# Batches in every eighth row: a decode block with x and biases in one transfer, merged VectorE copies and two weight pieces over eight DMA engines

## The chip, the cores and the metric

The kernel runs on one core of a Trainium2 chip. The metric is the time of one execution on the device in microseconds (us), lower is better. Before the change it is 214.59 us, the median of three runs (214.52 to 214.60).

## What is computed

One decode step of a transformer block, all in float32: attention over the last 1024 positions of a cache, with grouped query heads, and then an MLP, each behind a layer norm. The batch is B = 4, the model width D = 448, with 16 query heads on 8 key/value heads of 256, and F = 1792.

```python
def _A_ref(x, k_cache, v_cache, wq, wo):      # x: (4, 1, 448)
    W = min(4096, max(256, Sk // 4))          # 1024
    rep = Hq // Hkv                           # 2
    q = ((x @ wq).reshape(B, Sq, Hq, Dh)).transpose(0, 2, 1, 3)
    k = jnp.repeat(k_cache[:, :, Sk - W:, :], rep, axis=1)
    v = jnp.repeat(v_cache[:, :, Sk - W:, :], rep, axis=1)
    p = _softmax(jnp.einsum("bhqd,bhkd->bhqk", q, k) * (Dh ** -0.5), axis=-1)
    o = jnp.einsum("bhqk,bhkd->bhqd", p, v)
    return o.transpose(0, 2, 1, 3).reshape(B, Sq, Hq * Dh) @ wo

def _B_ref(x, w1, b1, w2, b2):
    y = _layernorm(x, axis=-1)
    h = _gelu(jnp.einsum("bsd,df->bsf", y, w1) + b1)
    return jnp.einsum("bsf,fd->bsd", h, w2) + b2

h = x + _A_ref(_layernorm(x, axis=-1), A_k_cache, A_v_cache, A_wq, A_wo)
h2 = h + _B_ref(_layernorm(h, axis=-1), B_w1, B_b1, B_w2, B_b2)
```

Some 88 MB are read for it: the windows of the two caches (67 MB) and the weights.

## The kernel before

**Tiles and stages.** The work goes by the eight key/value heads, called groups g0 to g7. For a group there is one k tile and one v tile of 128 partitions by 9984 floats: 8192 columns of cache, and behind them 1792 columns of weights, so that cache and weights come in one transfer. The k tile of group g carries the query weights of group g+1, the v tile the output weights of group g. Both kinds have two buffers (`ring`, line 37), so a load waits until the tile two before it is done with. The first v buffer takes `wq0` (the query weights of group 0, with x); the last k buffers take w1 and w2.

**A group's path.** `project_q` (L156) multiplies the normed x by the query weights and transposes the result (L165); VectorE reduces it and copies it to `qT` (L167, L173). `scores` (L175) multiplies `qT` with k into two halves of PSUM, VectorE takes the maxima (L186) and makes `nm`, the negative scaled maximum (L189, L190); ScalarE does the exponentials (L194). `transpose_p` (L203) turns them and VectorE copies them to `pT` (L211). `values` (L216) multiplies by v, `transposed_output` (L234) scales, transposes and folds the result into `oT` (L243, L244), and `add_output` (L246) adds the group's share of the output projection into `acc`. The main loop (L280 to L290) runs one group ahead with the scores.

**The tail.** From L293 on come the last group's value product in pieces, the residual and the two norms, the first MLP matmuls `pu` (L388), the gelu, and the second MLP: `pa` (L421) and `py` (L431). w2 comes in three pieces of 8, 4 and 2 row blocks; `py` starts with the second piece and ends with the third. `res` (L437) adds the residual, and one store writes the output. Matmuls on a zero tile (`keep_warm`) stand between them.

**Where batches lie.** PSUM results have four quadrants of 32 rows (Q = 32) for four concurrent matmuls. Of each quadrant only the first B = 4 rows hold a batch. The x rows and biases (`rs`, L129 to L133) are loaded into these rows by four transfers of 4 rows each, issued by ScalarE.

**The last 64 query rows.** The weights have 448 rows: three blocks of 128 and one of 64. In a packed weight tile the block of 64 rows by 512 columns stands as 128 rows by 256 columns. For group 1 alone it doesn't: k0 carries 1536 columns of weights, and the block comes in two transfers of 32 rows by 512 floats (L73) into `wq1_last`. Its source has 8 outer elements of four rows each, followed by padding, so that the outermost dimension of the transfer is 8.

**What sets the order.** PE's order is that of the code (`manual_schedule`). All bulk loads are issued by SyncE (SP) on one queue, q1, in the order of the program; a load waits for its buffer and for the semaphore lane that it takes over from an earlier transfer (eight lanes in turn, over both queues). ScalarE issues the `rs` rows on queue q10. Queues q8 and q14 fetch instructions.

Of the kernel before, what the change touches and what calls it, by code (L numbers as in the profile page):

```python
# [8 lines left out]
F32 = mybir.dt.float32  # L9
BF16 = mybir.dt.bfloat16  # L10
AF = mybir.ActivationFunctionType
ALU = mybir.AluOpType
# [14 lines left out]
Q = 32  # L27
CACHE = NKC * B * DH
WEIGHTS = 4 * D
EPS = 1e-5  # L30
SCALE = DH ** -0.5

@with_exitstack
def block_kernel(ctx: ExitStack, tc, rows, wq0, k0, wq1, kq, vo, w1, w2, out):
# [13 lines left out]
    def load(kind, src, pieces, name):  # L48
        t = ring.tile([P, CACHE + WEIGHTS], F32, tag=kind, name=name)
        at = 0  # L50
        for n in pieces:
            nc.sync.dma_start(t[:, at : at + n], src[:, at : at + n])  # L52
            at += n
        return t
# [8 lines left out]
        return parts  # L63


    def load_k(g):
        half = CACHE // 2
        if g == 0:
            t = load("k", k0, (CACHE + 3 * 512,), "k0")


            for i in range(2):
                nc.sync.dma_start(  # L73
                    wq1_last[i * Q : (i + 1) * Q, :], wq1[i].rearrange("e (p c) -> e p c", c=512)[:, :4, :]
                )
# [18 lines left out]
    ident = const.tile([P, P], F32, name="ident")  # L94
# [11 lines left out]

    yT = const.tile([P, ND + 1, Q], F32, name="yT")
    nc.vector.memset(yT, 0.0)
    wq1_last = const.tile([H, 512], F32, name="wq1_last")
    zT = const.tile([P, ND, Q], F32, name="zT")  # L110
    nc.vector.memset(zT, 0.0)

# [6 lines left out]
    rows_of = ident.rearrange("p (j q) -> p j q", j=4)[:, :, :B]  # L119
# [8 lines left out]

    rs = const.tile([P, 2 * P + FQ], F32, name="rs")  # L129
    nc.gpsimd.memset(rs, 0.0)  # L130
    for j in range(4):
        nc.scalar.dma_start(rs[j * Q : j * Q + B, :], rows[j])
    xb, b2b, b1b = rs[:, :P], rs[:, P : 2 * P], rs[:, 2 * P :]  # L133


# [20 lines left out]
    def project_q(g, parts):  # L156
        pq = ps_m.tile([P, 512], F32, tag="m", name=f"pq{g}")
        for j, y, cols, w in parts:
            nc.tensor.matmul(pq[j * Q : (j + 1) * Q, cols], y, w, start=True, stop=True)  # L159
        qs = work.tile([P, 512], F32, tag="qs", name=f"qs{g}")  # L160
        nc.scalar.copy(qs, pq)  # L161

        pt = ps_m.tile([P, 2 * REP, P], F32, tag="m", name=f"pqt{g}")
        for i in range(2 * REP):
            nc.tensor.transpose(pt[:, i, :], qs[:, i * P : (i + 1) * P], ident)  # L165
        sm = work.tile([P, 2 * REP, B], F32, tag="sm", name=f"sm{g}")
        nc.vector.tensor_reduce(  # L167
            sm, pt.rearrange("p i (j q) -> p i q j", j=4)[:, :, :B, :], axis=AX.X, op=ALU.add
        )

        src = sm.rearrange("p (r c) b -> p c b r", r=REP)
        for i in range(2):
            nc.vector.tensor_copy(qT[g % 2][:, :, :, i * REP : (i + 1) * REP], src)  # L173

    def scores(g, kt):  # L175
        mx = work.tile([P, 2], F32, tag="mx", name=f"mx{g}")
        halves = []
        for h in range(2):
            s = ps_s.tile([P, 512], F32, tag="s", name=f"s{g}_{h}")
            for c in range(2):  # L180
                for b in range(B):
                    nc.tensor.matmul(  # L182
                        s[b * Q : (b + 1) * Q, :], qT[g % 2][:, c, b, :], kt[h][:, c, b, :],
                        start=(c == 0), stop=(c == 1),
                    )
# [4 lines left out]
        nc.vector.tensor_scalar_mul(nm, nm, -SCALE)  # L190
# [12 lines left out]
    def transpose_p(g, p):  # L203
        for h in range(2):
            pt = ps_t.tile([P, 4, P], F32, tag="t", name=f"ppt{g}_{h}")
            for c in range(4):
                nc.tensor.transpose(pt[:, c, :], p[:, (4 * h + c) * P : (4 * h + c + 1) * P], ident)  # L207

            src = pt.rearrange("p (c i) (b q) -> p c i b q", i=2, b=B)
            for i in range(2):  # L210
                nc.vector.tensor_copy(  # L211
                    pT[g % 2][:, 2 * h : 2 * h + 2, :, i * REP : (i + 1) * REP], src[:, :, i, :, :REP]
                )


    def values(g, vt, po, pairs=range(NKC // 2)):  # L216
# [17 lines left out]
    def transposed_output(g, po, rec):  # L234
        o = work.tile([P, 2, DH], F32, tag="o", name=f"o{g}")
        nc.vector.tensor_scalar_mul(o, po, rec)  # L236
        pt = ps_m.tile([P, 2, 2, P], F32, tag="m", name=f"pot{g}")
        for i in range(2):
            for c in range(2):
                nc.tensor.transpose(pt[:, i, c], o[:, i, c * P : (c + 1) * P], ident)  # L240
        dst = oT[g % 2].rearrange("p (r c) q -> p c r q", r=REP)[:, :, :, :B]
# [51 lines left out]
    g = HKV - 2  # L293
# [88 lines left out]
    pu = ps_s.tile([P, 512], F32, tag="s", name="pu")[:, :FQ]  # L382
    pv = ps_m.tile([P, 2], F32, tag="m", name="pv")
    for a in range(ND):
        m = Q if a == 0 else B
        for j in range(4):
            rows, w = w1_part(a, j)
            nc.tensor.matmul(  # L388
                pu[j * Q : j * Q + m, :], zT[rows, a, :m], w, start=(a == 0), stop=(a == ND - 1),
            )  # L390
        if a == 0:
            rsqrt(r1, row_mean(dv, pv[:, 0:1], "v1"), "r1")
        if a == 1:
            v2 = stat("v2")
            nc.vector.tensor_scalar(v2, row_mean(zv, pv[:, 1:2], "v2"), r1, r1, op0=ALU.mult, op1=ALU.mult)
            rsqrt(s, v2, "r2")
            nc.vector.tensor_mul(s, s, r1)
# [10 lines left out]
    for rows in (slice(0, H), slice(H, P)):  # L408
        nc.tensor.matmul(put[rows, 3], u[:, 3 * P :], rows_of, start=True, stop=True)
    dst = gT[:, :12, :].rearrange("p (c j) q -> p c j q", c=3)  # L410
    nc.vector.tensor_copy(dst[:, :, :, :B], put[:, :3])

    for i, rows in enumerate((slice(0, H), slice(H, P))):
        nc.scalar.copy(gT[rows, 12:, :B], put[rows, 3].rearrange("p (j i) q -> p j i q", i=2)[:, :, i, :])
    keep_warm(1, warm)

    first = 8
    pa = ps_w.tile([P, D], F32, tag="acc", name="pa")
    for c in range(first):
        j, m = c % 4, Q if c < 4 else B  # L420
        nc.tensor.matmul(  # L421
            pa[j * Q : j * Q + m, :], gT[:, c, :m], w2t[c], start=(c < 4), stop=(c >= first - 4),
        )
    pas = once.tile([P, D], F32, tag="u", name="pas")
    nc.scalar.copy(pas, pa)
    py = ps_o.tile([P, 2, H], F32, tag="o", name="py")
    for c in range(first, NFC):
        for j in range(4):
            m, n = (Q, 2) if c == first else (B, 2 if j < 3 else 1)
            w = columns(w2t[c], j) if n == 2 else w2t[c][:, None, 3 * P :]  # L430
            nc.tensor.matmul(  # L431
                py[j * Q : j * Q + m, :n, :], gT[:, c, :m], w, start=(c == first), stop=(c == NFC - 1),
            )
        if c == first + 1:
            add_quadrants(py, pas, False)
# [69 lines left out]
```

## Time and profile before

| what | value |
|---|---|
| median time of three runs | 214.59 us |
| span of the profiled execution (first to last instruction) | 212.9 us |
| time that lies around that span | 1.69 us |
| PE busy | 137.9 us (65%) |
| VectorE (DVE) busy | 39.2 us (18%), 167 instructions |
| ScalarE (ACT) busy | 21.0 us (10%) |
| moved by DMA | 88.46 MB, mean 415 GB/s |
| mean granted TensorE clock | 0.872 |

The slices of the page cut the span into 40 parts of 5.3 us. A line of a group reads: source line, engine, operation, output<-input, shapes, count, then busy us and mean ns of one, then the idle time before them and what ended it. In a chain, the entry "DMA w<-w" is the time from what preceded it to the landing of that transfer. For each execution there is one span and the times of all queues' packets; the sixteen DMA engines are not told apart in any view.

### The profile page before, as it was taken

The page shows a single profiled execution, that of the slowest core. Times are in us where ns is not written, and L with a number is a line of the kernel's source. Part 1 is how long each engine was busy: PE and PEld are TensorE (multiplying, and loading weights), DVE is VectorE, ACT ScalarE, POOL GpSimd, SP SyncE. Part 2 cuts the span into 40 slices and gives each one's busy share as a digit, 9 for nine tenths or more (in the row PEclk, how much of TensorE's full clock was granted, in tenths as well). Part 3 has the DMA queues.
Part 4 walks back from the last instruction along what each step waited for, and adds up shares of the span by engine and source line. Part 5 has one row for each costly group of instructions (what it writes and reads, how often), then busy time and mean ns, then how long its engine had stood idle before and what let it go on. Part 6 is the DMA issues. An engine that isn't in the chain of part 4 may idle for free.

```text
span 212.9 us, 2306 instructions
## 1 busy us (share of the span) xinstructions
PE 137.9 (65%) x971; PEld 49.1 (23%) x971; DVE 39.2 (18%) x167; ACT 21.0 (10%) x52; POOL 5.6 (3%) x17
## 2 busy tenths in 40 slices
PE   0456868093886739583986348382948476798994
PEld 0322233021231212211231113120222123234432
DVE  1420324001130202210130104110230231022320
ACT  0210213000030000300030003000030001000311
POOL 6100000000000000000000000000000000000110
PEclk9999999669597966969599859979797999699999
DMA  7999998999989999999999999999989999999991
GB/s 291 426 399 469 398 465 378 459 465 390 458 378 465 465 390 458 398 446 465 390 458 405 443 465 386 465 413 428 461 375 468 440 428 390 417 418 433 424 390 60
DMA packets 3865, 88.46 MB, mean 415 GB/s; under 512 B 448, under 2 KB 576, under 8 KB 1168
## 3 DMA queue, kind: packets, MB, share of 16 engines
q1 hardware_dynamic: 3824, 88.29, 96.9%
q8 instruction: 7, 0.11, 0.2%
q10 hardware_dynamic: 32, 0.05, 0.1%
q14 instruction: 2, 0.02, 0.0%
HBM read 88.26 MB, written 0.07 MB: 415 GB/s over the span
## 4 chain that ended last, share of the span: by engine, by line
DMA 85%; PE 11%; DVE 2%; issue 0%; SPq 0%
DMA v<-vo 65%; DMA w<-w 12%; DMA k<-k 8%; PE po L219 8%; PE acc L248 1%; DVE o L236 1%; PE pot L240 1%; PE py L431 1%; DVE oT L243 0%; DVE oT L244 0%; SPq L52 0%; DVE res L437 0%; PE py L256 0%
## 5 line engine op out<-in xcount | busy, mean ns | idle before, releaser
L182 PE MATMUL s<-k,qT 128*32 128x512 f32 x256 | 42.3, 822 | 24.7 <-DMA k<-kq 22.6
L219 PE MATMUL po<-v,pT 128*32 128x512 f32 x256 | 40.0, 772 | 19.6 <-DMA v<-vo 19.6
L186 DVE TENSOR_REDUCE mx<-s 128x1 f32<-128x512 f32 x16 | 11.1, 691 | 67.4 <-PE s L182 67.4
L182 PEld LDWEIGHTS s<-k,qT 128*32 128x32 f32 x256 | 10.0, 146 | 54.7 <-issue 29.4
L219 PEld LDWEIGHTS po<-v,pT 128*32 128x32 f32 x256 | 10.7, 135 | 42.3 <-issue 31.4
L161 ACT COPY qs<-pq 128x512 f32<-128x512 f32 x8 | 4.7, 586 | 135.8 <-PE pq L159 135.8
L236 DVE TENSOR_SCALAR o<-po,rec 128x512 f32<-128x512 f32 x8 | 6.0, 750 | 60.2 <-PE po L219 60.2
L194 ACT ACTIVATE p<-s,nm 128x512 f32<-128x512 f32 x16 | 10.9, 690 | 18.4 <-DVE nm L190 18.4
L207 PE MATMUL ppt<-ident,p 128*128 128x128 f32 x64 | 10.5, 286 | 2.0 <-ACT p L194 1.7
L165 PE MATMUL pqt<-ident,qs 128*128 128x128 f32 x32 | 5.7, 304 | 6.2 <-ACT qs L161 6.2
L240 PE MATMUL pot<-ident,o 128*128 128x128 f32 x32 | 5.2, 286 | 5.7 <-DVE o L236 5.7
L248 PE MATMUL acc<-v,oT 128*32 128x448 f32 x56 | 6.7, 551 | 3.3 <-DVE oT L244 3.3
L207 PEld LDWEIGHTS ppt<-ident,p 128*128 128x128 f32 x64 | 6.7, 140 | 6.0 <-ACT p L194 6.0
L159 PE MATMUL pq<-k,yT 128*32 128x512 f32 (+1 forms) x66 | 7.3, 515 | 0.0
L308 PE MATMUL warm<-idle 128*32 128x512 bf16 x25 | 7.3, 382 | 0.0
L240 PEld LDWEIGHTS pot<-ident,o 128*128 128x128 f32 x32 | 3.3, 140 | 13.0 <-DVE o L236 13.0
L165 PEld LDWEIGHTS pqt<-ident,qs 128*128 128x128 f32 x32 | 3.6, 150 | 10.9 <-ACT qs L161 9.1
L153 POOL TENSOR_TENSOR r<-ve_r,mhalf 128x1 f32<-128x1 f32 x2 | 1.1, 544 | 191.9 <-DVE ve_r L152 191.9
L211 DVE COPY pT<-ppt 128x16 f32<-128x16 f32 x32 | 4.7, 170 | 4.7 <-PE ppt L207 4.7
L159 PEld LDWEIGHTS pq<-k,yT 128*32 128x32 f32 x66 | 3.1, 110 | 6.1 <-issue 4.8
L138 PE MATMUL pm_x<-wq,mean 128*128 128x12 f32 x2 | 0.6, 363 | 5.8 <-DMA wq<-wq 5.8
L167 DVE TENSOR_REDUCE sm<-pqt 128x16 f32<-128x64 f32 x8 | 1.8, 225 | 13.0 <-PE pqt L165 13.0
(101 smaller groups left out, 60.9 us busy)
## 6 DMA issues: line engine op xcount, KB each, us to landing
v<-vo SPq DMA_DIRECT2D x7, 4992.0 KB, 31.8
k<-kq SPq DMA_DIRECT2D x6, 4992.0 KB, 32.0
k<-k SPq DMA_DIRECT2D x1, 4864.0 KB, 16.3
k<-kq SPq DMA_DIRECT2D x1, 4096.0 KB
w<-w SPq DMA_DIRECT2D x2, 1792.0 KB
v<-vo SPq DMA_DIRECT2D x2, 1024.0 KB, 22.2
v<-vo SPq DMA_DIRECT2D x1, 2048.0 KB
w<-w SPq DMA_DIRECT2D x1, 1344.0 KB
```

The lines of the kernel that those rows point to most:

```text
L159: nc.tensor.matmul(pq[j * Q : (j + 1) * Q, cols], y, w, start=True, stop=True)
L161: nc.scalar.copy(qs, pq)
L165: nc.tensor.transpose(pt[:, i, :], qs[:, i * P : (i + 1) * P], ident)
L182: nc.tensor.matmul(s[b * Q : (b + 1) * Q, :], qT[g % 2][:, c, b, :], kt[h][:, c, b, :], start=(c == 0), stop=(c == 1),)
L186: nc.vector.reduce_max(mx[:, h : h + 1], s, axis=AX.X)
L194: nc.scalar.activation(p[:, h * 512 : (h + 1) * 512], halves[h], AF.Exp, bias=nm, scale=SCALE, accum_out=sums[:, h : h + 1],)
L207: nc.tensor.transpose(pt[:, c, :], p[:, (4 * h + c) * P : (4 * h + c + 1) * P], ident)
L219: nc.tensor.matmul(po[b * Q : (b + 1) * Q], pT[g % 2][:, c, b, :], vt[c][:, :, b, :], start=(c == 0), stop=(c == NKC // 2 - 1),)
L236: nc.vector.tensor_scalar_mul(o, po, rec)
L240: nc.tensor.transpose(pt[:, i, c], o[:, i, c * P : (c + 1) * P], ident)
L248: nc.tensor.matmul(acc[i * Q : (i + 1) * Q, :], oT[g % 2][:, i, :], wt[:, i, :], start=(g == 0), stop=(g == HKV - 2),)
L308: nc.tensor.matmul(warm[:Q], idle[:, :Q], idle, start=True, stop=True)
```

## The change

Batch b now lies in row 8b of its quadrant instead of row b (STEP = 8), for `rs`, `oT`, `zT`, `gT`, and the selection from `ident`. With that, the sixteen rows of x and biases are one regular transfer. `qT`, `nm` and `pT` are made with one VectorE instruction where there were two. In the tail, matmuls that used 4 columns of weights use 32. And the last 64 query rows of group 2 leave k1 and come like those of group 1, through an outermost dimension of 8.

```diff
@@ load_k
+    def load_last(n):
+        t = wq_last[:, n, :]
+        for i in range(2):
+            nc.sync.dma_start(
+                t[i * Q : (i + 1) * Q, :], wql[n, i].rearrange("e (p c) -> e p c", c=512)[:, :4, :]
+            )
+        return t
...
-            last = wq1_last
+            last = load_last(0)
+        elif g == 1:
+            t = load("k", kq[0], (CACHE + 3 * 512,), "k1")
+            last = load_last(1)
...
-    for j in range(4):
-        nc.scalar.dma_start(rs[j * Q : j * Q + B, :], rows[j])
+    nc.scalar.dma_start(rs[::STEP, :], rows)
@@ project_q, scores, transpose_p
-        src = sm.rearrange("p (r c) b -> p c b r", r=REP)
-        for i in range(2):
-            nc.vector.tensor_copy(qT[g % 2][:, :, :, i * REP : (i + 1) * REP], src)
+        src = sm.rearrange("p (r c) b -> p c b r", r=REP)[:, :, :, None, :].to_broadcast([P, 2, B, 2, REP])
+        nc.vector.tensor_copy(qT[g % 2][:, :, :, : 2 * REP].rearrange("p c b (i r) -> p c b i r", i=2), src)
...
-        nc.vector.tensor_max(nm, mx[:, 0:1], mx[:, 1:2])
-        nc.vector.tensor_scalar_mul(nm, nm, -SCALE)
+        nc.vector.tensor_scalar(nm, mx[:, 0:1], mx[:, 1:2], -SCALE, op0=ALU.max, op1=ALU.mult)
...
-            src = pt.rearrange("p (c i) (b q) -> p c i b q", i=2, b=B)
-            for i in range(2):
-                nc.vector.tensor_copy(
-                    pT[g % 2][:, 2 * h : 2 * h + 2, :, i * REP : (i + 1) * REP], src[:, :, i, :, :REP]
-                )
+            src = pt.rearrange("p (c i) (b q) -> p c b i q", i=2, b=B)[:, :, :, :, :REP]
+            dst = pT[g % 2][:, 2 * h : 2 * h + 2, :, : 2 * REP]
+            nc.vector.tensor_copy(dst.rearrange("p c b (i r) -> p c b i r", i=2), src)
@@ the rows of a batch, here zT; oT, gT and rows_of likewise
-    nc.vector.tensor_copy(zT[:, :, :B], pz)
+    nc.vector.tensor_copy(zT[:, :, ::STEP], pz)
@@ the tail, here pu; pa and py likewise
-        m = Q if a == 0 else B
...
-                pu[j * Q : j * Q + m, :], zT[rows, a, :m], w, start=(a == 0), stop=(a == ND - 1),
+                pu[j * Q : (j + 1) * Q, :], zT[rows, a, :], w, start=(a == 0), stop=(a == ND - 1),
```

On SyncE, the first loads of the program before were these; `wq` is group 0's weights with x, a lane is named DMAHW with its number, and PE and DVE stand for a wait for a buffer's readers:

```order
L52 DMA wq_134<-wq 128x1808
L52 DMA k_174<-k 128x9728
L73 DMA wq_last<-wq 32x1x512 x2
L52 DMA k_239<-kq 128x9984 [waits DMAHW0_49]
L52 DMA v_241<-vo 128x9984 [waits DMAHW1_49]
L52 DMA k_335<-kq 128x9984 [waits DMAHW2_49,PE_49]
L52 DMA v_337<-vo 128x9984 [waits DMAHW3_49,DVE_49]
```

And now:

```order
L53 DMA wq_131<-wq 128x1808
L53 DMA k_170<-k 128x9728
L70 DMA wq_last<-wql 32x1x512 x2
L53 DMA k_231<-kq 128x9728
L70 DMA wq_last<-wql 32x1x512 x2
L53 DMA v_235<-vo 128x9984 [waits DMAHW0_49]
L53 DMA k_324<-kq 128x9984 [waits DMAHW1_49,PE_49]
L53 DMA v_326<-vo 128x9984 [waits DMAHW2_49,DVE_49]
```

Two transfers have moved in between k1 and v0, k1 has 256 columns less and waits for no lane, and v0 waits for the lane of `wq0` instead of that of k0.

On VectorE, the work between two groups' maxima, here of group 1, before:

```order
L189 TENSOR_TENSOR nm_264<-mx_243 128x1
L190 TENSOR_SCALAR nm_264<-nm_264 128x1
L167 TENSOR_REDUCE sm_287<-pqt_282 128x16
L173 COPY qT_111<-sm_287 128x8x2 x2
L211 COPY pT_114<-ppt_0_291 128x8x2
L199 TENSOR_TENSOR rec_271<-sums_268 128x1
L211 COPY pT_114<-ppt_0_291 128x8x2
L200 RECIPROCAL rec_271<-rec_271 128x1
L211 COPY pT_114<-ppt_1_298 128x8x2 x2
```

And now:

```order
L196 TENSOR_SCALAR nm_258<-mx_237 128x1
L175 TENSOR_REDUCE sm_279<-pqt_274 128x16
L180 COPY qT_111<-sm_279 128x8x4
L217 COPY pT_114<-ppt_0_282 128x8x4
L205 TENSOR_TENSOR rec_264<-sums_261 128x1
L206 RECIPROCAL rec_264<-rec_264 128x1
L217 COPY pT_114<-ppt_1_288 128x8x4
```

Eleven instructions (two rows stand for two each) have become seven, in the same order.

On PE, the last matmuls of the tail kept their number and order; the weights of `py` before and now, in the first rows:

```order
L431 MATMUL py<-w_827,gT 32x128 x4
L431 MATMUL py<-w_827,gT 4x128 x3
L431 MATMUL py<-w_827,gT 4x64
L256 MATMUL py<-pas,sel 32x128 x4
L431 MATMUL py<-w_827,gT 4x128 x3
L431 MATMUL py<-w_827,gT 4x64
```

```order
L434 MATMUL py<-w_796,gT 32x128 x7
L434 MATMUL py<-w_796,gT 32x64
L260 MATMUL py<-pas,sel 32x128 x4
L434 MATMUL py<-w_796,gT 32x128 x3
L434 MATMUL py<-w_796,gT 32x64
```

Only the width of a weight tile has changed, from 4 to 32 columns.

More of the change, by code (lines that the diff above doesn't have):

```diff
@@ L27 @@
 Q = 32
+STEP = Q // B
 CACHE = NKC * B * DH
@@ L33, in block_kernel @@
 @with_exitstack
-def block_kernel(ctx: ExitStack, tc, rows, wq0, k0, wq1, kq, vo, w1, w2, out):
+def block_kernel(ctx: ExitStack, tc, rows, wq0, k0, wql, kq, vo, w1, w2, out):
     nc = tc.nc
@@ L108, in block_kernel @@
     nc.vector.memset(yT, 0.0)
-    wq1_last = const.tile([H, 512], F32, name="wq1_last")
+    wq_last = const.tile([H, 2, 512], F32, name="wq_last")
     zT = const.tile([P, ND, Q], F32, name="zT")
@@ L118, in block_kernel @@
     fold = fold.rearrange("p j q -> p (j q)")
-    rows_of = ident.rearrange("p (j q) -> p j q", j=4)[:, :, :B]
+    rows_of = ident.rearrange("p (j q) -> p j q", j=4)[:, :, ::STEP]
     qT = [const.tile([P, 2, B, Q], F32, name=f"qT{i}") for i in range(2)]
@@ L410, in block_kernel @@
     dst = gT[:, :12, :].rearrange("p (c j) q -> p c j q", c=3)
-    nc.vector.tensor_copy(dst[:, :, :, :B], put[:, :3])
+    nc.vector.tensor_copy(dst[:, :, :, ::STEP], put[:, :3])
     for i, rows in enumerate((slice(0, H), slice(H, P))):
-        nc.scalar.copy(gT[rows, 12:, :B], put[rows, 3].rearrange("p (j i) q -> p j i q", i=2)[:, :, i, :])
+        nc.scalar.copy(gT[rows, 12:, ::STEP], put[rows, 3].rearrange("p (j i) q -> p j i q", i=2)[:, :, i, :])
     keep_warm(1, warm)
@@ L419, in block_kernel @@
     for c in range(first):
-        j, m = c % 4, Q if c < 4 else B
+        j = c % 4
         nc.tensor.matmul(
-            pa[j * Q : j * Q + m, :], gT[:, c, :m], w2t[c], start=(c < 4), stop=(c >= first - 4),
+            pa[j * Q : (j + 1) * Q, :], gT[:, c, :], w2t[c], start=(c < 4), stop=(c >= first - 4),
         )
@@ L428, in block_kernel @@
         for j in range(4):
-            m, n = (Q, 2) if c == first else (B, 2 if j < 3 else 1)
+            n = 2 if c == first or j < 3 else 1
             w = columns(w2t[c], j) if n == 2 else w2t[c][:, None, 3 * P :]
             nc.tensor.matmul(
-                py[j * Q : j * Q + m, :n, :], gT[:, c, :m], w, start=(c == first), stop=(c == NFC - 1),
+                py[j * Q : (j + 1) * Q, :n, :], gT[:, c, :], w, start=(c == first), stop=(c == NFC - 1),
             )
@@ L488 @@
     rows = np.concatenate([quadrants(xp), quadrants(b2), quadrants(np.asarray(B_b1).reshape(1, F))], axis=2)
+    rows = rows.reshape(4 * B, 2 * P + FQ)
     arrays = {
-        "rows": rows, "wq0": np.concatenate([wq[0], xT], axis=1), "k0": k0, "wq1": wq1, "kq": kq, "vo": vo, "w1": w1, "w2": w2,
+        "rows": rows, "wq0": np.concatenate([wq[0], xT], axis=1), "k0": k0, "wql": wql, "kq": kq, "vo": vo, "w1": w1, "w2": w2,
     }
@@ L502 @@
     r = run(nc, [arrays], core_ids=[0])
-    got = np.asarray(r.results[0]["out"]).reshape(4, Q, P)[:, :B, :]
+    got = np.asarray(r.results[0]["out"]).reshape(4, B, STEP, P)[:, :, 0]
     return np.ascontiguousarray(got.transpose(1, 0, 2).reshape(B, 1, 4 * P)[:, :, :D])
```

10 lines of the change are left out of this document (3 added, 7 removed).

## The prediction

> **What bounds the kernel now.** I read the page's busy shares and slices first, then the queues, then the chain.
>
> ```profile
> span 212.9 us, 2306 instructions
> DMA  7999998999989999999999999999989999999991
> q1 hardware_dynamic: 3824, 88.29, 96.9%
> q8 instruction: 7, 0.11, 0.2%
> q10 hardware_dynamic: 32, 0.05, 0.1%
> q14 instruction: 2, 0.02, 0.0%
> DMA 85%; PE 11%; DVE 2%; issue 0%; SPq 0%
> ```
>
> The sixteen DMA engines are busy in every slice from the second to the last but one, and 85% of the chain that ended last is DMA. SyncE's queue q1 alone fills 96.9% of the sixteen engines' span. One engine therefore moves 88.29 MB / (0.969 x 16 x 212.9 us) = 26.7 KB per us; I use that rate for every small transfer below. The instruction queues and q10 (ScalarE's, the `rs` rows) take little.
>
> Next, whether this stream ever starves. These are stretches of the span: length, busy time of PE, PEld, DVE, ACT, POOL, granted clock, DMA share, GB/s. After them come two DMA groups with their KB and the us from issue to landing.
>
> ```profile
> 17.40:29.80 12.40, 9.61 (x52) 3.14 (x52) 2.87 (x13) 1.94 (x5) 0.00 (x0) 1.00 0.97 419
> 29.80:66.00 36.20, 22.65 (x152) 7.98 (x152) 6.83 (x29) 3.87 (x10) 0.00 (x0) 0.81 1.02 437
> 66.00:113.00 47.00, 32.46 (x196) 10.22 (x196) 7.92 (x32) 3.87 (x10) 0.00 (x0) 0.78 1.00 433
> 113.00:160.00 47.00, 27.86 (x196) 9.09 (x196) 7.93 (x32) 3.87 (x10) 0.00 (x0) 0.85 1.00 428
> 182.10:205.50 23.40, 21.35 (x180) 8.48 (x180) 5.16 (x19) 3.31 (x8) 1.09 (x2) 0.93 1.01 422
> v<-vo SPq DMA_DIRECT2D x7, 4992.0 KB, 31.8
> k<-kq SPq DMA_DIRECT2D x6, 4992.0 KB, 32.0
> ```
>
> The share is 0.97 to 1.02 throughout (packets are booked where they start, hence above 1). A load of 4992 KB needs 5.11 MB / 430 GB/s = 11.9 us, yet lands 32 us after its issue: some 20 us of other loads stand before it. So a wait of SyncE or a faster VectorE changes nothing in the stream while it is shorter than that. What counts is the work of the DMA engine that finishes last, and what follows it:
>
> ```profile
> 206.50:207.00 0.50, 0.50 (x8) 0.13 (x4) 0.00 (x0) 0.03 (x1) 0.00 (x0) 1.00 0.92 380
> 207.00:207.50 0.50, 0.50 (x12) 0.13 (x4) 0.00 (x0) 0.00 (x0) 0.00 (x0) 1.00 0.75 308
> 207.50:208.00 0.50, 0.50 (x8) 0.00 (x0) 0.00 (x0) 0.00 (x0) 0.00 (x0) 1.00 0.61 244
> 208.00:208.50 0.50, 0.13 (x7) 0.09 (x8) 0.00 (x0) 0.35 (x1) 0.00 (x0) 1.00 0.60 244
> 208.50:209.00 0.50, 0.50 (x24) 0.50 (x28) 0.00 (x0) 0.18 (x1) 0.00 (x0) 1.00 0.17 65
> 182.14 26.22 DMA w<-w
> 208.41 0.64 PE py L431 x13
> 209.22 0.97 PE py L431 x19
> 210.21 0.29 DVE res L437
> PE py L431 <- DMA w<-w: 0.4, 1, 0.4
> ```
>
> Sixteen times the share is the number of engines still at work: 14.7, 12.0, 9.8, 9.6, 2.7. So about six engines are through by 207.5 us, and nine or ten finish together about 1 us later. The idle time in these rows is (0.08 + 0.25 + 0.39 + 0.40 + 0.83) x 0.5 = 0.98 us per engine: perfect balance would bring the last engine that much forward, no more. Behind it comes a fixed tail. PE stands 0.4 us for the second-last piece of w2, runs 1.7 us of `py`, then `res` follows.
>
> Why two groups? q8 carries seven packets of 16 KB (PE's instructions). Its 0.2% (0.15 to 0.25) of 16 x 212.9 us is 5.1 to 8.5 us, 0.7 to 1.2 us a packet. Seven such packets and q14's two make nine delays of about 1 us at most, and nine or ten engines are late. No view names an engine. That the q8 packets sit on the eight engines that `wq_last` does not use is a guess, and the sign of the sum below hangs on it: on the other eight they would make rival 2.
>
> **The change, part by part.**
>
> *The last 64 query rows of group 2.* k1 loses 256 columns x 4 B x 128 rows = 131,072 B, or 8,192 B on each of sixteen engines: -8.2/26.7 = -0.31 us. The same bytes come back over eight engines, 16,384 B each: +0.61 us. Net: eight "high" engines -0.31, eight "low" ones +0.30.
>
> *x and biases.* 16 rows of 2,816 B. I take four transfers of four rows to have used four engines (one row each, four times), and one of 16 rows to use all sixteen. A packet costs 2.8/26.7 = 0.11 us; q10's 0.1% (0.05 to 0.15) over 16 data packets bounds it by 0.11 and 0.32. I take 0.11, which agrees with the rate. If the four are engines 0 to 3, they go from 0.44 to 0.11; the others gain 0.11.
>
> Sum per engine: 0 to 3: +0.30 - 0.33 = -0.03; 4 to 7: +0.30 + 0.11 = +0.41; 8 to 15: -0.31 + 0.11 = **-0.20** (between -0.31 and +0.01).
>
> *SyncE and ScalarE.* Two more issues stand between k1 and v0, and the waits shift.
>
> ```profile
> L73 SPq DMA_DIRECT2D wq_last<-wq x2: 682/750/819, 1.6 to 2.5; - x2
> L132 ACTq DMA_DIRECT2D rs<-rows x4: 260/316/557, 4.1 to 5.3; - x4
> 5.68 0.34 SPq L52 DMA_DIRECT2D k<-kq  x1
> 17.46 0.33 SPq L52 DMA_DIRECT2D v<-vo  x1
> ```
>
> k1 no longer waits for wq0's landing (5.68 us) and v0 no longer for k0's (17.46); v0 waits for wq0 instead. Two issues of 0.75 us ahead of it on SP are covered: v0's bytes start only when k1's are through, near 29.8 us (an end of one of the stretches above). ScalarE saves three issues of 0.3 us ahead of its table load, under its wait for the first projection. Both: 0. Without the cover, 1.5 us later v0, once.
>
> *VectorE.* Groups of instructions, mean ns of one, then the idle time before them:
>
> ```profile
> L182 PE MATMUL s<-k,qT 128*32 128x512 f32 x256 | 42.3, 822 | 24.7 <-DMA k<-kq 22.6 <-DMA k<-k 2.1
> L211 DVE COPY pT<-ppt 128x16 f32<-128x16 f32 x32 | 4.7, 170 | 4.7 <-PE ppt L207 4.7
> L173 DVE COPY qT<-sm 128x16 f32<-128x16 f32 x16 | 2.0, 172 | 0.3
> L190 DVE TENSOR_SCALAR nm<-nm 128x1 f32<-128x1 f32 x8 | 1.2, 154 | 0.3
> L395 DVE TENSOR_SCALAR v<-pv,r 128x1 f32<-128x1 f32 x1 | 0.3, 276 | 1.1 <-PE pv L349 1.1
> L411 DVE COPY gT<-put 128x48 f32<-128x48 f32 x1 | 0.2, 208 | 1.3 <-PE put L409 1.3
> ```
>
> 16 pT copies, 8 qT copies and 8 `nm` steps go. A merged copy has 32 elements, between the 170 ns of 16 and the 208 of 48; the merged `nm` costs 154 to 276 ns. Per group that is at most 0.6 us off VectorE. PE then waits as much longer for k (24.7 us already): 0. Were PE the bound, eight groups would give up to 4.8 us.
>
> *Strided writes and 32 columns in the tail.* The copies to zT, oT and gT keep their element counts: 0. The weights of `pu`, `pa` and `py` grow from 4 to 32 columns.
>
> ```profile
> 199.54 0.96 PE L388 MATMUL pu<-w,zT 128*32 128x448 f32 x8
> 200.75 0.94 PE L388 MATMUL pu<-w,zT 128*4 128x448 f32 x8
> L431 PEld LDWEIGHTS py<-w,gT 128*4 128x4 f32 x40 | 1.1, 86 | 0.1
> L431 PEld LDWEIGHTS py<-w,gT 128*32 128x32 f32 x8 | 0.2, 108 | 1.2 <-DMA w<-w 1.2
> ```
>
> Eight matmuls take 0.96 against 0.94 us, so a weight load of 108 instead of 86 ns hides behind the matmul. Ahead of `py` PE's 0.4 us of waiting covers it; inside `py` it is 0 to 5 x 0.02 = 0.10 us. I take 0, since the stream there is paced by the matmuls in the same way.
>
> **A page's rule against it.** The Trainium skill, "DMA: Bandwidth & Descriptors", section "Rules for kernel authors", says that an outermost dimension below 16 confines a DMA to that many engines, and wants a multiple of 16 there; its section on the semaphore adds that the lowest-numbered engines are taken. By the rows above, engines end 1 us apart, so more load on some need not delay the last. If all ended together, as that rule assumes, the low eight's +0.30 would be the result; this is the fourth case below.
>
> **The sum.** The last engine moves by -0.20, the tail by 0: span 212.7 us. The profiled execution's 212.9 us lies 1.69 us below the median of 214.59, time outside the span that I keep. Forecast **214.39 us**.
>
> **Rivals.**
> 1. *The last engine is one of 0 to 3* (a q14 delay on an engine that also carries rows). For: nine or ten are late, and the high half has only eight, so one or two late ones are low. Against: these may end early in the 208.50 row. It moves by -0.03: 214.56.
> 2. *The last becomes one of 4 to 7.* Same evidence for; it decides if the late low engine carries no rows and ends within 0.4 us of the last. Price +0.41 to +0.62: 215.0 to 215.2, slower.
> 3. *More than balance moves.* 32 VectorE instructions fewer may spare one of q14's two packets. If that one sat on the last engine, the next ones decide: 2.7 of 9.6 busy puts the mean end at 208.5 + 0.5 x 2.7/9.6 = 208.64, 0.3 us before the last, and these move by -0.20 as well: -0.5, 214.09. Against: nine late engines make it unlikely that none is close behind the last.
> 4. *The change does not relieve an end*, because low and high end together: +0.30, 214.89.
>
> **How the numbers follow.** Forecast 0.42; rivals 0.10, 0.17, 0.25, 0.06. 0.2% is 0.43 us, about what a measurement of this kernel can tell from no change. Within it lie the forecast and rivals 1 and 4: 0.58; faster is rival 3: 0.25; slower is rival 2: 0.17. The forecast's own range is 214.25 to 214.65 (0 to 0.10 of `py`, -0.31 to +0.01 of the high half). The whole range runs from rival 3 with a rounded edge, 214.0, to the near end of rival 2, 215.0, and leaves out about 0.1.
>
> **What would show it.** Right: the early and the late group of engines end closer together, and `py` starts on w2 about 0.2 us earlier. PE's waits for k and v grow by what VectorE saves. Wrong: a gap in the DMA share after 17 us (the waits of v0 or k2), a `py` longer than 1.8 us, PE no longer waiting for w2, or q8 with other than seven packets.

## The result, and the profile after

The changed kernel takes **215.11 us** (median of 7 runs, 214.97 to 215.23) against 214.59 us (7 runs, 214.36 to 214.69): ratio 1.0027, 95% interval 1.0018 to 1.0036, or +0.52 us. The forecast was 214.39 us with a range to 215.0. The profiled execution took 214.97 us, 1.79 us of it around its span. In the fifteen traces of the experiments below that difference is 1.78 to 1.88 us, with one of 2.15; so the 1.69 us that the prediction reckoned between the span of before and its median means that this profile of before was about 0.1 us above its median.

The page of the changed kernel: span, VectorE, the slices, the queues, the chain by engine.

```profile
span 213.2 us, 2268 instructions
PE 136.1 (64%) x969; PEld 48.1 (23%) x969; DVE 37.4 (18%) x135; ACT 21.0 (10%) x52; POOL 5.6 (3%) x17
DMA  7999899999999999999999999999999999999991
q1 hardware_dynamic: 3904, 88.29, 96.8%
q8 instruction: 7, 0.11, 0.2%
q10 hardware_dynamic: 32, 0.05, 0.1%
q14 instruction: 2, 0.02, 0.0%
DMA 87%; PE 9%; DVE 2%; issue 0%; SPq 0%
```

The stream is as full as before, with the same bytes in 80 packets more. VectorE has 32 instructions and 1.8 us less. PE waits 27.9 us for k (24.7 before) and 17.6 us for v (19.6 before), 1.2 us more in all, so most of what VectorE saves goes into waiting for DMA. The rows of the two products now, and that of v before:

```profile
L189 PE MATMUL s<-k,qT 128*32 128x512 f32 x256 | 43.5, 842 | 27.9 <-DMA k<-kq 25.8
L223 PE MATMUL po<-v,pT 128*32 128x512 f32 x256 | 35.1, 694 | 17.6 <-DMA v<-vo 17.6
L219 PE MATMUL po<-v,pT 128*32 128x512 f32 x256 | 40.0, 772 | 19.6 <-DMA v<-vo 19.6
```

Both instruction queues carry what they carried. The difference is at the end. These are the stretches of 0.5 us in which the last engines finish (the DMA share stands before GB/s).

```profile
206.50:207.00 0.50, 0.47 (x8) 0.28 (x12) 0.00 (x0) 0.00 (x0) 0.00 (x0) 1.00 0.95 387
207.00:207.50 0.50, 0.50 (x12) 0.22 (x8) 0.00 (x0) 0.00 (x0) 0.00 (x0) 1.00 0.81 330
207.50:208.00 0.50, 0.50 (x8) 0.00 (x0) 0.00 (x0) 0.00 (x0) 0.00 (x0) 1.00 0.71 287
208.00:208.50 0.50, 0.24 (x4) 0.00 (x0) 0.00 (x0) 0.15 (x1) 0.00 (x0) 1.00 0.43 172
208.50:209.00 0.50, 0.38 (x17) 0.38 (x21) 0.00 (x0) 0.39 (x1) 0.00 (x0) 1.00 0.05 22
209.00:209.50 0.50, 0.50 (x30) 0.50 (x21) 0.00 (x0) 0.00 (x0) 0.00 (x0) 1.00 0.02 7
```

The end of the chain (start, duration, what):

```profile
181.94 26.63 DMA w<-w
208.62 0.64 PE py L434 x13
209.26 0.17 PE py L260 x6
209.43 0.97 PE py L434 x19
210.43 0.29 DVE res L440
```

Times sixteen, the shares are 15.2, 13.0, 11.4, 6.9, 0.8 and 0.3 engines on average: more engines than before are busy until 208.0, then they end together, and **one engine** works on alone past 209.0. `py` starts at 208.62 us where it started at 208.41, and from there to `res` the kernel takes 1.81 us where it took 1.80. So the time is lost in front of `py`, by the last DMA engine.

SyncE's first issues, from its timeline (start, duration, line):

```profile
3.20 0.44 SPq L53 DMA_DIRECT2D k<-kq  x1
3.68 1.43 SPq L70 DMA_DIRECT2D wq_last<-wql  x2
5.44 0.33 SPq L53 DMA_DIRECT2D v<-vo  x1
```

k1, its extra piece and v0 go out at 3.2 to 5.8 us, early enough, as the prediction had it. Now the queues in the stretch from 203 to 206 us alone (packets, MB, share of the sixteen engines):

```profile
q1 hardware_dynamic: 145, 1.19, 95.7%
q8 instruction: 1, 0.02, 2.1%
```

The last of the seven instruction packets falls into the stretch from 203 to 206 us; its own time is 2.1% of 16 x 3 us, 1.0 us.

**Which engine is it?** No view names one, but the times of the packets do: each engine takes one packet after the other, so a packet belongs to the engine whose last packet ended just before, and the 2 KB packets mark the eight engines that `wq_last` uses ("low" in the prediction). All eight engines of a half take the same sequence of packet sizes, which settles most places where two ends fall together. Put together in this way, the changed kernel's trace reads as follows; only the engines that end at 207.92 and 208.44 us could stand the other way round. The loss is the time by which an engine's other packets are delayed around an instruction packet.

```
engine   end of last packet   instruction packet (its end), loss
low      207.67 207.73 207.76 207.88 207.92   none
low      208.45               202.1 (q14) 0.68
low      208.61               44.0  (q14) 0.97
low      209.18               204.8 (q8)  1.55
high     206.55 206.86        none
high     208.19 208.22 208.35 208.43 208.44 208.48   one q8 each, 1.55 (35 to 187)
```

Low engines without an instruction packet end at 207.7 to 207.9 us, the two high ones at 206.55 and 206.86: some 1.1 us apart, where two pieces of 16 KB are 1.2 us at 26.7 KB per us. A packet of PE's instructions costs its engine 1.55 us: it takes 1.0 to 1.1 us itself, and the data packet behind it, of 39 KB, 1.97 us instead of 1.48. Six of seven fell on high engines, which have the room; the seventh fell on a low one, and that is the straggler.

**And before the change?** Read in the same way, before's trace has the last q8 packet (it ends at 203.6 us) on a low engine that carries no x rows, and this engine ends last, at 208.97 us. A low engine without a packet ends at 207.32, and 207.32 + 1.55 = 208.87. The trace of e8 below, whose transfers are those of before, reads alike: a low engine with the q8 packet of 203.4 us ends last, at 208.82. So the last engine was a low one already, and bytes added to the low half push the end out. Between the two traces that end moves by 0.21 us only, but before's profile lay 0.1 us above its median and the changed kernel's 0.14 below, which makes 0.45.

### The profile page after: what moved, and what is told of

Same layout as the page of the kernel before. It is cut to its first block, busy times and chain, and to the rows that moved or that the text cites. A ratio compares the mean times of both kernels' runs of the same rounds, so it can differ in the third digit from the quotient of the medians.

```text
span 213.2 us, 2268 instructions
## 1 busy us (share of the span) xinstructions
PE 136.1 (64%) x969; PEld 48.1 (23%) x969; DVE 37.4 (18%) x135; ACT 21.0 (10%) x52; POOL 5.6 (3%) x17
## 4 chain that ended last, share of the span: by engine, by line
DMA 87%; PE 9%; DVE 2%; issue 0%
DMA v<-vo 73%; DMA w<-w 12%; PE po L223 6%; DMA wq<-wq 2%; PE acc L252 1%; DVE o L240 1%; PE pot L244 1%; PE py L434 1%; DVE oT L247 0%; DVE oT L248 0%; DVE res L440 0%; PE py L260 0%
## 5 line engine op out<-in xcount | busy, mean ns | idle before, releaser
L189 PE MATMUL s<-k,qT 128*32 128x512 f32 x256 | 43.5, 842 | 27.9 <-DMA k<-kq 25.8
L223 PE MATMUL po<-v,pT 128*32 128x512 f32 x256 | 35.1, 694 | 17.6 <-DMA v<-vo 17.6
L223 PEld LDWEIGHTS po<-v,pT 128*32 128x32 f32 x256 | 8.9, 125 | 38.0 <-issue 23.9
L391 PE MATMUL pu<-w,zT 128*32 128x448 f32 (+1 forms) x32 | 3.8, 550 | 0.4 <-DMA w<-w 0.4
## 6 DMA issues: line engine op xcount, KB each, us to landing
w<-w SPq DMA_DIRECT2D x2, 1792.0 KB, 27.9
```

The lines of the kernel that those rows point to most:

```text
L189: nc.tensor.matmul(s[b * Q : (b + 1) * Q, :], qT[g % 2][:, c, b, :], kt[h][:, c, b, :], start=(c == 0), stop=(c == 1),)
L223: nc.tensor.matmul(po[b * Q : (b + 1) * Q], pT[g % 2][:, c, b, :], vt[c][:, :, b, :], start=(c == 0), stop=(c == NKC // 2 - 1),)
```

## The experiments

Each kernel ran beside before on the same chip, and its ratio is taken against those runs. The theory is rival 2 of the prediction: the last engine is a low one, so the piece adds its +0.30 us. Its rivals: the forecast's own rule (the last engine is a high one); the tail; and one that came out of the traces. After the output is stored, SyncE waits for the semaphore lanes one after the other in a fixed order, 62 ns each; the order of the transfers decides on which of eight lanes the store lies, and so how many of these waits come behind its landing.

### The parts of the change by themselves

**e1: before, with only the last 64 query rows of group 2 over eight engines.**

```diff
+        elif g == 1:
+            t = load("k", kq[0], (CACHE + 3 * 512,), "k1")
+            for i in range(2):
+                nc.sync.dma_start(
+                    wq2_last[i * Q : (i + 1) * Q, :], wq2[i].rearrange("e (p c) -> e p c", c=512)[:, :4, :]
+                )
+            last = wq2_last
...
```

> The kernel before with only the last 64 query rows of group 2 taken out of k1 and sent over eight DMA engines; all else as before. Engine theory: the DMA engine that ends last is one of the eight low ones, because a late instruction packet falls on it; it gets 16,384 B more and 8,192 B less, +0.30 us, so 214.9 us, and at the end of the span a single engine is still at work. Tail theory (the slowdown comes from the strided writes, the 32-column weights or the merged copies): 214.6 us, unchanged. High-half theory of the prediction (the last engine is a high one): 214.3 us.

Measured: 215.03 us against 214.54 (ratio 1.0019, interval 1.0010 to 1.0027). Its end, the stretches first and then the chain:

```profile
207.50:208.00 0.50, 0.50 (x8) 0.00 (x0) 0.00 (x0) 0.00 (x0) 0.00 (x0) 1.00 0.66 265
208.00:208.50 0.50, 0.28 (x8) 0.06 (x8) 0.00 (x0) 0.17 (x1) 0.00 (x0) 1.00 0.31 122
208.50:209.00 0.50, 0.50 (x20) 0.38 (x24) 0.00 (x0) 0.36 (x1) 0.00 (x0) 1.00 0.11 43
```

```profile
208.44 0.64 PE py L439 x13
```

Slower, so the forecast's -0.31 for the high half does not reach the end. But `py` starts at 208.44, hardly later than in before's profile, while the span is 0.2 us longer: the rest stands behind the output (the lanes, below).

**e14: the same kernel a second time**, on another chip.

> The kernel of e1_eight_only a second time, beside e13 and e15 on one chip: 215.03 as the first time. Its waits behind the output's landing (lane 1) are 0.19 us by the records of e1.

Measured: 215.01 us against 214.49 (1.0015 to 1.0035); `py` starts at 208.45. In both traces the last engine is a low one, though not by a q8 packet: it carries x rows and the q14 packet of 38.5 us (40.0 in e14), and ends at 209.04 (209.02). In e14 the low engine with the last q8 packet ends just before it, at 208.99. So this program kept its straggler on another chip.

**e2: the changed kernel, with k1 loaded whole.**

```diff
-        elif g == 1:
-            t = load("k", kq[0], (CACHE + 3 * 512,), "k1")
-            last = load_last(1)
```

> The changed kernel with k1 whole again, so without the second piece over eight engines; rows in one transfer, merged copies, every eighth row stay. Engine theory: the last engine loses 0.30 us against the changed kernel, 214.8 us; the high half comes up by 0.31 us and ends close behind. Tail theory: as the changed kernel, 215.1 us. High-half theory: 215.4 us.

Measured: 214.87 us against 214.54 (1.0006 to 1.0024). Without the piece the kernel is 0.24 us faster than the changed one (0.19 if each is taken against its own before) and still slower than before.

**e8: before, with only the merged VectorE copies** (`qT`, `nm`, `pT` as in the diff of the change).

> The kernel before with only the merged VectorE instructions (qT, nm, pT); all transfers, rows and lanes as before. Engine theory and prediction: no change, 214.55 us, since loads end last. If the shorter program or other waits move something: a difference over 0.1 us either way.

Measured: 214.55 us against 214.59 (0.9992 to 1.0010). The merged copies are worth nothing here, as predicted.

**e3: the changed kernel, with the sixteen rows in four transfers of four.**

```diff
-    nc.scalar.dma_start(rs[::STEP, :], rows)
+    for j in range(4):
+        nc.scalar.dma_start(rs[j * Q : (j + 1) * Q : STEP, :], rows[j * B : (j + 1) * B])
```

> The changed kernel with the 16 rows of x and biases in four transfers of four rows again (into every eighth row), everything else as changed. If the last engine is one that the four transfers do not use (4 to 15), it is spared one packet: -0.1 us, 215.0 us. If it is one of those four, it gets three packets more: +0.33 us, 215.4 us. Tail theory: 215.1 us.

Measured: 215.21 us against 214.54 (1.0019 to 1.0041). That is 0.10 above the changed kernel, or 0.15 if each is taken against its own before; the lanes (below) make 0.12. Whether the four engines carry the rows or all sixteen makes no difference that can be told at the end.

**e7: the changed kernel, with the last rows of group 3 over eight engines too** (`elif g <= 2`, and a third piece in `wql`).

> The changed kernel with the last 64 query rows of group 3 over eight engines too (the suspected cost once more). Engine theory: +0.30 us for the low eight, and the output's lane goes from 6 to 0, one or two more waits at the end (+0.06 to +0.13): 215.5 us, with the low engines alone at work at the end. Tail theory: 215.15 us.

Measured: 215.60 us against 214.59 (1.0034 to 1.0059), 0.49 over the changed kernel. Its last stretches show the low engines pulled out further, about two of them past 209.0 and one past 209.5; behind the stretches the row of the chain:

```profile
208.50:209.00 0.50, 0.38 (x5) 0.00 (x0) 0.00 (x0) 0.01 (x1) 0.00 (x0) 1.00 0.22 86
209.00:209.50 0.50, 0.32 (x12) 0.32 (x16) 0.00 (x0) 0.50 (x1) 0.00 (x0) 1.00 0.14 57
209.50:210.00 0.50, 0.50 (x29) 0.49 (x25) 0.00 (x0) 0.02 (x1) 0.00 (x0) 1.00 0.04 14
```

```profile
209.18 0.64 PE py L434 x13
```

The two last engines are low ones, each with a q8 packet (of 36.0 and 71.8 us). So each piece of that kind pushes the end out again, which is the theory's sign; on the forecast's rule it would have gained once more.

### The instruction packets

**e4: the changed kernel, with only the first of four pairs of value matmuls in the first six groups** (the other three are left out).

```diff
-        values(g, vt, po)
+        values(g, vt, po, range(1), 0)
...
```

> The changed kernel with a quarter of the value matmuls in the first six groups (only the first pair of key blocks, so the output is not the reference's); every load stays. PE then runs some 290 instructions fewer, enough to drop its last instruction packet of 256. Engine theory: q8 carries six packets instead of seven, the single late engine at the end of the span is gone, -0.6 us against the changed kernel: 214.5 us. Tail theory, or a theory in which the packets do not matter: 215.1 us.

Measured: 215.11 us against 214.54 (1.0016 to 1.0038): a miss. Its page and its last stretches:

```profile
span 213.2 us, 1980 instructions
q8 instruction: 6, 0.10, 0.2%
```

```profile
208.50:209.00 0.50, 0.33 (x13) 0.34 (x16) 0.00 (x0) 0.49 (x1) 0.00 (x0) 1.00 0.16 65
209.00:209.50 0.50, 0.50 (x30) 0.50 (x25) 0.00 (x0) 0.00 (x0) 0.00 (x0) 1.00 0.04 14
```

One packet is gone, but the others came at other times, and by the packets' times two of the six now lie on low engines (near 115 and 154 us), and these two end late, where one did. So the engine on which a packet falls changes with the program, and this shortening gained nothing. By its time alone the run does not tell the theories apart.

### The lanes

**e5: before, with three transfers of 64 bytes** ahead of everything else on ScalarE's queue, which turn the output's lane from 7 to 2.

```diff
+    tiny = const.tile([1, 3, 16], F32, name="tiny")
+    for j in range(3):
+        nc.scalar.dma_start(tiny[:, j, :], rows[0, 0:1, 16 * j : 16 * (j + 1)])
```

> The kernel before with three tiny transfers of 64 bytes on ScalarE's queue, which nothing reads: they only turn the eight semaphore lanes, so that the store of the output stands on lane 2 instead of lane 7. Lane theory: SyncE ends the program with one wait after the other in the order of the lanes, 62 ns each, and the waits behind the output's lane (none before, four to five now) come after the landing: +0.25 to +0.31 us, 214.8 us. If these waits are hidden: 214.55 us.

Measured: 214.80 us against 214.59 (1.0002 to 1.0020). `py` starts at 208.28, even earlier than in before, so the loss is behind it. The tails of all runs show it. "Waits" are SyncE's waits recorded behind the landing of the output, and the lane is read from the order of the program:

```
kernel                     lane  waits  py starts   span    span - py   median - before
before                       7     0     208.41    212.92     4.51          -
e8  merged copies            7     0     208.27    212.76     4.49        -0.04
e15 small transfers only     7     0     208.23    212.76     4.53        +0.11
e5  small transfers, lane 2  2     4     208.28    213.01     4.73        +0.21
e10 no piece, lane 7         7     0     208.39    212.88     4.49        +0.21
e2  no piece                 4     3     208.46    213.16     4.70        +0.33
after                        6     1     208.62    213.18     4.56        +0.52
e4  fewer matmuls            6     1     208.67    213.22     4.55        +0.57
e3  rows in four             1     3     208.80    213.47     4.67        +0.67
e1  piece only               1     3     208.44    213.14     4.70        +0.49
e14 piece only, again        1     3     208.45    213.14     4.69        +0.52
e12 piece only, lane 7       7     0     208.68    213.18     4.50        +0.71
e13 piece only, lane 7       7     0     209.02    213.56     4.54        +0.96
e7  three pieces             0     2     209.18    213.79     4.61        +1.01
```

From `py`'s start to the end it takes 4.49 to 4.54 us without such a wait, 4.55 or 4.56 with one, 4.61 with two, 4.67 to 4.70 with three, 4.73 with four: about 0.06 us each. The changed kernel has one, +0.06 us; e1 and e2 have three, +0.19 us.

**e10: e2 with three such transfers**, back on lane 7.

> The kernel of e2_no_eight (after, with k1 loaded whole as before) with three transfers of 64 bytes on ScalarE's queue, which turn the output store's lane from 4 to 7. What is left of its +0.33 is then the rows' packet (2.8 KB on each of sixteen engines instead of on four), and merged copies and strided writes at nothing: +0.11 if the last engine gains a row packet and nothing else counts, 214.65 to 214.70 with 214.55 before. If e2's +0.33 was not lanes: 214.87 again. If the rows cost nothing either: 214.55.

Measured: 214.74 us against 214.53 (1.0001 to 1.0019). What the change does apart from the piece and the lanes costs +0.21 us by this pair, +0.14 by e2 without its lanes. The merged copies are nothing by e8. The rows over sixteen engines are the one transfer that differs: the last engine of before carries none of them and gains one packet, 0.11 us, which lies within the interval (0.02 to 0.41). But e3, with the rows back on four engines, does not gain it back, so that the rows do it is not shown.

### The piece on lane 7

**e9: e1 with six small transfers at the start.**

> The kernel of e1_eight_only (before, with the last 64 query rows of group 2 over eight engines and nothing else) with six transfers of 64 bytes on ScalarE's queue, which turn the output store's semaphore lane from 1 back to 7, where nothing is waited for behind its landing. Engine theory (a low DMA engine ends last, and it carries 0.30 us more): +0.30 over before, 214.85 to 214.95, and no recorded SyncE waits behind the output's landing. The forecast's rule (the last engine is a high one and loses 0.31): -0.25, 214.3. If e1's +0.49 was the piece alone and the lanes nothing: +0.49, 215.05.

Measured: 217.60 us against 214.53 (1.0126 to 1.0157). SyncE's issues and the stretch from 12 to 18 us:

```profile
1.18 0.41 SPq L52 DMA_DIRECT2D k<-k  x1
11.29 3.91 SPq L73 DMA_DIRECT2D wq_last<-wq  x2
17.42 0.34 SPq L52 DMA_DIRECT2D k<-kq  x1
```

```profile
12.00:18.00 6.00, 2.52 (x17) 1.12 (x13) 0.48 (x3) 0.59 (x1) 0.00 (x0) 1.00 0.66 280
```

With twelve transfers wanting eight lanes, SyncE stood until 11.29 us for a lane, k1 went out at 17.42 instead of 5.36, and the stream ran dry: (1 - 0.66) x 6 = 2.0 us of the 3.1 (the traced run itself took 219.43 us). It shows a gap in the DMA share, the sign of being wrong that the prediction named, and not the price of the piece.

**e11: the same with the six transfers written at the end of the first six groups.** Nothing held them there, and they were again issued at the start.

> The kernel of e1_eight_only again with six transfers of 64 bytes, but one at the end of each of the first six groups instead of six at the start, so that the output store is back on lane 7 and no load near the start waits for a lane. Engine theory (a low DMA engine ends last and carries 0.30 us more; the other 0.19 of e1's +0.49 were waits behind the output's landing): +0.30, 214.85 to 214.95 with 214.55 before. If e9's +3.1 us was a cost of small transfers as such and not of the starved stream from 12 to 18 us: over 217 again. If lanes are nothing: 215.05, as e1.

Measured: 217.51 us against 214.61 (1.0122 to 1.0156), again a share of 0.66 from 12 to 18 us. The same stall, so no answer.

**e12: the six held to their groups** by copying from that group's probabilities (`p[0:1, ...]` as their source).

> e11_eight_spread again, but each of the six transfers of 64 bytes now takes its data from the probabilities of a group, so that it can not be issued at the program's start: in e11 all six were, and SyncE stood until 11.2 us for a lane, with a DMA share of 0.66 from 12 to 18 us. The start is e1's, the output store is on lane 7. Engine theory plus lanes: +0.30, 214.85 to 214.95 with 214.55 before, no recorded SyncE waits behind the output's landing, DMA share 0.97 or more from 12 to 18 us. If lanes are nothing, or small transfers cost something as such: 215.05 or more. The forecast's rule (the last engine is a high one): 214.3.

Measured: 215.24 us against 214.53 (1.0021 to 1.0048). The start is whole, no waits are left behind the output, and yet it is slower than e1. But its padding is heavy: 224 packets on q10 against 32.

**e13: the six read contiguous bytes**, one packet each, and are held to their groups by a copy into their target.

```diff
+        nc.vector.tensor_copy(tiny[:, g, :], p[0:1, 16 * g : 16 * (g + 1)])
+        nc.scalar.dma_start(tiny[:, g, :], first_rows[0, 0:1, 16 * g : 16 * (g + 1)])
```

> e12_eight_lane7b again, but its six small transfers read 64 contiguous bytes of DRAM, one packet each, and are held to their groups by a 16-element copy into their target just ahead of them (in e12 the six made 180 packets more than in e1). The eight-engine piece of e1 with the output store on lane 7. Engine theory: +0.30 over before, 214.85 to 214.95 with 214.55 before; 0.1 to 0.2 under e14_eight_again of the same call. If lanes are nothing: the same as e14. The forecast's rule: 214.3.

**e15: before, with eight of these transfers**, the padding alone.

> Before with eight such 64-byte transfers, two at the end of each of the first two groups and one at the end of each of the next four, so that the output store stays on lane 7: what the transfers cost by themselves. Expected nothing that can be measured: 214.55 to 214.65. If each costs an engine its time like a 16 KB instruction packet, or holds up a load through its lane: 214.8 or more, and then e13 has to be read against this run.

Measured: e13 215.45 us, e15 214.60 us, both against 214.49 (1.0029 to 1.0056; 0.9994 to 1.0011). The padding costs nothing that can be told, the waits behind the output are gone, and yet the kernel is 0.44 us slower than e14, the piece without padding on the same chip. The last stretches of e13 and its chain:

```profile
208.50:209.00 0.50, 0.29 (x4) 0.00 (x0) 0.00 (x0) 0.10 (x1) 0.00 (x0) 1.00 0.27 108
209.00:209.50 0.50, 0.48 (x18) 0.36 (x18) 0.00 (x0) 0.44 (x1) 0.00 (x0) 1.00 0.13 50
```

```profile
182.51 26.47 DMA w<-w
209.02 0.64 PE py L443 x13
```

The expectation of 214.9 is missed, and not by the lanes: `py` starts at 209.02 us, 0.58 later than in e1, with the same bytes in the same shapes. Two engines on average are busy past 209.0 (0.13 x 16). Read as above, the two last engines of e13 are low ones with a q8 packet each (of 189.7 and 205.8 us; they end at 209.40 and 209.60): two of seven lie on low engines, where e14 has one. e12 has two as well (189.5 and 204.3). But low engines with no rows and no packet end later too, at 207.8 us in e13 against 207.4 to 207.7 in e14, so the packets are not all of it. That part is open.

### One transfer for the piece

**e6: before, with the pieces of groups 1 and 2 over eight engines, each as one transfer of 64 rows** instead of two of 32.

```diff
-            for i in range(2):
-                nc.sync.dma_start(
-                    wq1_last[i * Q : (i + 1) * Q, :], wq1[i].rearrange("e (p c) -> e p c", c=512)[:, :4, :]
-                )
+            nc.sync.dma_start(wq1_last, wq1.rearrange("e (p c) -> e p c", c=512)[:, :8, :])
...
+            nc.sync.dma_start(wq2_last, wq2.rearrange("e (p c) -> e p c", c=512)[:, :8, :])
...
```

> The kernel before with the last 64 query rows of groups 1 and 2 over eight DMA engines, each in one transfer of 64 rows instead of two of 32: as many transfers as before, so the output's lane is 7 as before and nothing stands behind it. Engine theory: the last engine, a low one, gets +0.30 us: 214.85 us. If the slowdown of the run with two transfers each came from the lanes alone: 214.55 us.

Measured: 216.15 us against 214.59 (1.0064 to 1.0090): a miss by 1.3 us. The stretch in which the second piece is read, in e6 and then in e1:

```profile
28.00:31.00 3.00, 0.51 (x8) 0.29 (x9) 0.41 (x4) 0.00 (x0) 0.00 (x0) 1.00 1.09 376
```

```profile
28.00:31.00 3.00, 1.36 (x16) 0.57 (x20) 0.21 (x2) 0.00 (x0) 0.00 (x0) 1.00 1.20 510
```

The engines are nearly as busy and move a quarter less: 2 KB packets take a median of 105 ns there instead of 84, and the 39 KB packets that start from 28.1 to 30.9 us take 1.6 to 2.0 us instead of 1.5. That is 0.4 MB less, some 0.9 us at 430 GB/s. Why it reads slower was not tried; the run says nothing on the theory.

## Why the prediction was wrong

Taken apart by the table, the +0.52 us are: the piece of group 2 about +0.3 (e1 and e14 without their lanes +0.30 and +0.33; the changed kernel less e2, both without lanes, +0.32), the rest of the change +0.14 to +0.21 (argued to be the rows, not shown), one wait behind the output +0.06. Merged copies and the tail are 0.

- **The step that failed** is "That the q8 packets sit on the eight engines that `wq_last` does not use is a guess, and the sign of the sum below hangs on it". The last engine was taken for a high one, moved by -0.20. In before's own trace it is a low one without x rows, the engine with the last q8 packet (208.97 us), and in every trace that was read in this way (before, after, e1, e2, e3, e4, e7, e8, e10, e12 to e15) a low engine ends last. It is the kind of engine of rival 2, whose price of +0.41 with one lane makes +0.47 of the measured +0.52; the sum was done rightly on both sides, and the chance of 0.17 was the error. Most q8 packets did sit on high engines, six of seven in the changed kernel, but an end is set by the worst engine: one packet on a more loaded engine is enough, and all seven would have had to miss them.
- The delay of an instruction packet was put at 0.7 to 1.2 us from its queue's share. Its own time is 1.0 to 1.1 us; the engine loses 1.55 us, as the packet beside it waits too. That late engines are those with such a packet, as the prediction reasoned, is borne out by the reading above: the nine that end at 208.19 us or later are the nine with one. The Trainium skill, "Runtime: NRT & Kernel Launch", section "Instruction fetch mechanics", calls the cost of crossing a 16 KiB block mostly hidden; that may hold for the engine that fetches, but here a DMA engine pays, and one of them sets the end.
- The bytes per engine were right: low and high engines without instruction packets end some 1.1 us apart in the changed kernel, near twice the 0.61 us of one piece. The fourth rival (low and high engines end together) has the price of the low half, +0.30, but not its premise: the ends are spread from 206.6 to 209.2 us. The rule of the Trainium skill beside it, "DMA: Bandwidth & Descriptors", section "Rules for kernel authors", to keep a multiple of 16 outermost, holds here: e1 and e7 lose by breaking it. That all engines end together is the prediction's reading of it; the section does not say so.
- Rows: one of sixteen rows uses sixteen engines, and its sixteen packets, one each, end at 8.8 to 9.5 us; before, they came four at a time until 16.9 us, on four engines. The relief of -0.33 for four engines did not show at the end: with four transfers again (e3) the time is that of the changed kernel but for the lanes, so rival 1's last engine among these four is not borne out for the changed kernel.
- VectorE, SyncE's issues, 32 columns and strided writes at 0: right (e8; `py` to `res` 1.81 against 1.80 us; no gap in the stream). Rival 3 fell: q14 still has two packets.
- What the sum did not have: the order of the transfers moves the output's lane, +0.06 us here and up to +0.25.

**Still open:** e12 and e13 carry the same bytes as e1 and end 0.24 to 0.58 us later in front of `py`. Each has a second q8 packet on a low engine, but their low engines without one end later too, for which no cause was found. So "+0.3 us for a piece" holds for this program, and by e12 and e13 another may pay 0.7 to 1.0. Open too is whether the +0.14 to +0.21 beside the piece are the rows.

## What to carry to other kernels

Where all DMA engines are full to the end, count the bytes of each engine and add the packets of instructions: what moves load from sixteen engines to eight is a loss unless the last engine is known to be one of the other eight, and a mean end says nothing about that. Whoever changes the number or order of transfers also moves semaphore lanes: with eight of them, a ninth early transfer can stop the issuing queue for microseconds, and the place of the last store changes the end by 0.06 us a lane.

## What the runs showed of the hardware

- A 16 KB packet of instructions takes 1.0 to 1.1 us itself and costs the DMA engine that it falls on 1.55 us; one of 8 KB costs 0.7 to 1.0 us.
- At the end of the program SyncE's waits for lanes cost 62 ns each, one after the other, and those behind the output's landing lie bare.
- One transfer of 64 rows slowed the packets beside it too, for some 3 us (376 GB/s at a DMA share of 1.09, in e6), where two of 32 did not (510 GB/s, in e1).
